# V through float32 staging buffers, K turned before Q with gated turns, and a later zeroing: what they do to a sliding-window attention and MoE kernel

## The chip, the cores and the metric

The kernel runs on one core of a Trainium2 chip. The metric is device time in microseconds (us) from the first to the last instruction, as a median over several executions. An execution is called slow when it is more than 1.5% above the fastest of the same kernel. The medians below are over all executions, a few slow ones included (348.79 us beside 343.3 us of the kernel before is one by this rule).

TensorE is PE in the profile (PEld is its weight load), VectorE is DVE, ScalarE is ACT, GpSimd is POOL and SyncE is SP.

## The reference

```python
# q, k, v: [8 batches, 8 heads, 576, 64] float32; window 32 to either side
scores = (q @ k.T) / sqrt(64);  scores[abs(i - j) > 32] = -1e9
attn   = softmax(scores)
x      = (attn @ v) -> transposed to [4608 tokens, 512]
# the "MoE" part is one dense block: w_in [512, 2048], w_out [2048, 512]
out    = (max(x @ w_in, 0) ** 2) @ w_out          # [4608, 512] float32
```

## The kernel before

A recorder takes every operation with its engine, its reads and writes, an estimated duration and a priority (`key`). A list scheduler then fixes one order for each engine, and semaphores are put in from the dependencies. **On the chip each engine's list is run in the order in which it stands**, whatever the scheduler believed about durations (in the traces of the kernels before and after, the instructions of all five engines stand in the order of their lists, by source line; in the kernel after, ACT's first casts of V come 1st, 2nd, 9th, 12th, 14th and 25th, as in its list).

Each batch of 576 positions is done in nine chunks of 64 queries. Batches 0 and 1 are fed by fine pieces, which PE transposes; ACT evicts Q and DVE evicts K. From batch 2 on, GpSimd loads Q and K raw, with a cast to bfloat16; DVE "turns" them (32x32 transposes), and SP's DMAs "spread" the turned data into the layout for the scores. V goes into `VD`. The half-shifted copy `VX`, which even chunks need, is made from `VD` by SP's DMAs; the edges of `VX` come from HBM.

```python
# ---- the scheduler's idea of a DMA (cut) ----
if op.dma is not None:
    q = "SW" if e == "POOL" else "HW"
    moved[q] = max(moved[q], t + op.dur + 700) + op.move
    if q == "HW":
        moved["SW"] += op.move          # the other way round nothing is added
    op.end = moved[q] + 1300

# ---- V: GpSimd issues DMAs that cast float32 to bfloat16 ----
def load_v(self, b, key, s):                        # four large pieces of a batch
    i = b % 2
    self.p.rec("POOL", lambda e, s=s: e.dma_start(
        self.VD[i][:, s, :, 0:64], v[b, :, 32 + 128 * s:160 + 128 * s, :].rearrange("h p d -> p h d")),
        writes=[("vd", i, s)], dma=(f"v{i}{s}", b), key=key, dur=900, move=2050)

def load_ve(self, b, key, hi):                      # the two edges of a batch
    ...                                             # three forms of the same: into VX, from POOL

def copy_v(self, b, key, s0, s1):                   # VX from VD, by SP's DMAs
    self.p.rec("SP", ... self.VX[i][0:64, s0 + 1:s1 + 1] <- self.VD[i][64:128, s0:s1] ...)

# ---- the turns of batch b (cut); raw buffers and VD/VX alternate with b % 2 ----
if b > 1:
    self.load_qk(b, "q", kb); self.load_qk(b, "k", kb)   # POOL, into RAW[t][b % 2]
    ...
    for st in range(8):
        t, dh, m = ("q", "k")[st // 4], st // 2 % 2, st % 2
        self.turn(b, t, dh, 5 * m, 5 + 4 * m, 9 * b - LEAD - TOFF + st * TST + (5 if b == 2 else 0),
                  [self.masked[min(9 * b - TREL + st, 9 * b - 1) if b > 2 else 12 + st // 2]])
        if st % 4 == 3:
            self.spread(b, t, 9 * b - LEAD - 9)          # SP
    self.copy_v(b, 9 * b - LEAD - 6, 0, 4)

# ---- zeroing for batch 1, early ----
self.setup_rest(1, -40)
self.setup_qz(1, -30, [(0, 64, 0), (64, 64, 1)])
```

The last argument of `turn` is an order constraint: a turn may not come before a given softmax mask in DVE's order. We call it the old hold.

The softmax here doesn't subtract the row's maximum and nothing guards it: scores larger than these inputs give would overflow.

## Time and profile before

The kernel took 346.15 us (median of three runs, 343.3 to 348.79).

| stretch of the profiled run | PE idle |
|---|---|
| 0 to 75 us | 21.4 us |
| 80 to 130 us | 7.5 us |
| whole span, 345.2 us | 32.9 us |

PE idle is length less PE busy in the tables of stretches. Only this idle time, the clock and the work itself can change the length, as PE, busy for 312.3 of 345.2 us, bounds the kernel.

These lines are from the page of the kernel before: busy time by engine; three rows of the picture in 40 slices, where a digit is the busy share in tenths (PEclk is the granted TensorE clock in tenths); the queues; and the chain that ended last.

```profile
PE 312.3 (90%) x2736; PEld 183.1 (53%) x2736; DVE 204.8 (59%) x468; ACT 180.9 (52%) x349; POOL 82.8 (24%) x130
...
PE   1457699999989679998999999999999999999996
...
PEclk9995689999999899999999999999999999999999
DMA  8999999965996996987997474542200000010012
...
q0 software_dynamic: 62272, 18.49, 56.7%
q1 hardware_dynamic: 14400, 20.71, 20.4%
...
PE 78%; DVE 10%; DMA 6%; ACT 3%; issue 2%; SPq 0%; ACTq 0%
```

Counting slices of 8.6 us from 0, PE has holes in slices 0 to 4, between 10 and 14 and a small one in 18, and none from slice 19 to the last but one. DMA is at 90% or more for most of the first 60 us. The table of stretches of the same kernel gives lengths, then each engine's busy us, the clock and the DMA share (the time of the packets as a share of 16 engines' time; as printed it can exceed 1). The trace holds no clock record before 20.99 us; the tables print 1.00 for that time.

```profile
core 0: us, PE busy (x) PEld busy (x) DVE busy (x) ACT busy (x) POOL busy (x), PEclk, DMA share, GB/s
0.00:20.00 20.00, 8.19 (x112) 6.84 (x112) 13.27 (x46) 7.71 (x13) 18.75 (x37) 1.00 1.21 147
20.00:40.00 20.00, 11.15 (x143) 9.47 (x144) 9.44 (x22) 9.82 (x19) 14.10 (x21) 0.70 1.49 200
40.00:60.00 20.00, 19.83 (x316) 16.57 (x315) 10.74 (x28) 11.57 (x23) 7.13 (x11) 0.88 2.35 161
```

Two places in the chain, read in order of time (start, length, what), looked worth attacking: PE's scores of batches 2 and 3 each stand after a spread of K of 7 us. These are the lines of batch 2; batch 3's spread takes 7.35 us from 116.18 us on.

```profile
93.80 7.14 DMA kt<-kst
...
101.07 0.61 PE sc L411 x8
```

Lastly the waits (who waited for whom: us in total, times, longest). GpSimd waits a lot for PE to free V's buffers, yet no engine waits for GpSimd's own work, except PE for the identity matrix at the start (5.9 us). PE waits only 1.0 us for the shifted V, `vx<-vd`.

```profile
engine line waited for: us in total, times, longest us
POOL vd L313 <- PE avp L439: 60.6, 12, 8.3
...
PE sc L411 <- DMA kt<-kst: 3.7, 2, 2.1
...
PE avp L438 <- DMA vx<-vd: 1.0, 1, 1.0
```

### The profile page before, as it was taken

To read this page: it belongs to the slowest core of one execution; us is meant where nothing else is said; L and a number is where in the kernel's file an instruction comes from. 1 tells how busy PE (TensorE), PEld (TensorE's weight loads), DVE (VectorE), ACT (ScalarE), POOL (GpSimd) and SP (SyncE) were. 2 spreads that over 40 slices of the span, in tenths; PEclk is the share of its full clock that TensorE was granted. 3 is DMA by queue.
4 is the path that set the end of the run, shared out by engine and by line. 5 is a ranking of instruction groups with operands and counts; after the bars stand their busy time and mean duration, and the time that the engine had idled before them with its cause. 6 is when DMAs were issued, how large, how long until landed. Compare 5 with 4: busy or idle time off the path is not lost.

```text
span 345.2 us, 6957 instructions
## 1 busy us (share of the span) xinstructions
PE 312.3 (90%) x2736; PEld 183.1 (53%) x2736; DVE 204.8 (59%) x468; ACT 180.9 (52%) x349; POOL 82.8 (24%) x130
## 2 busy tenths in 40 slices
PE   1457699999989679998999999999999999999996
PEld 1346398776845345544555555555555555444442
DVE  7634556869949857796886676777544444222200
ACT  2365258883536368555565555555555555544421
POOL 8999115102415424141341111100000000000000
PEclk9995689999999899999999999999999999999999
DMA  8999999965996996987997474542200000010012
GB/s 93 185 192 211 171 149 184 208 79 99 218 213 82 243 145 67 123 122 164 176 207 118 80 167 89 85 127 66 65 32 30 34 30 32 30 61 32 30 61 91
DMA packets 76703, 39.63 MB, mean 115 GB/s; under 512 B 41856, under 2 KB 71168, under 8 KB 76672
## 3 DMA queue, kind: packets, MB, share of 16 engines
q0 software_dynamic: 62272, 18.49, 56.7%
q1 hardware_dynamic: 14400, 20.71, 20.4%
q8 instruction: 21, 0.34, 0.4%
q14 instruction: 10, 0.08, 0.1%
HBM read 36.96 MB, written 9.44 MB: 134 GB/s over the span
## 4 chain that ended last, share of the span: by engine, by line
PE 78%; DVE 10%; DMA 6%; ACT 3%; issue 2%; SPq 0%; ACTq 0%
PE outp L529 32%; PE ht L511 26%; PE ht L488 7%; PE sc L411 5%; DMA kt<-kst 4%; DVE kst L366 3%; PE avp L438 3%; PE trp L467 3%; PE avp L439 3%; DMA vx<-vd 2%; DVE qz L204 2%; ACT qz L292 1%; DVE kt L295 1%; PE sc L276 1%; DVE xr L456 1%
## 5 line engine op out<-in xcount | busy, mean ns | idle before, releaser
L529 PE MATMUL outp<-w,gt 128*128 128x512 bf16 x576 | 144.8, 382 | 0.0
L511 PE MATMUL ht<-xt,w 128*128 128x512 bf16 x448 | 115.2, 383 | 0.2 <-ACT xt L471 0.2
L517 ACT ACTIVATE rt<-ht 128x512 bf16<-128x512 f32 x112 | 67.1, 599 | 69.6 <-PE ht L511 67.1
L529 PEld LDWEIGHTS outp<-w,gt 128*128 128x128 bf16 x576 | 54.2, 98 | 57.6 <-issue 1.6
L519 DVE TENSOR_TENSOR gt<-rt 128x512 bf16<-128x512 bf16 x112 | 46.6, 418 | 43.8 <-ACT rt L517 43.3
L511 PEld LDWEIGHTS ht<-xt,w 128*128 128x128 bf16 x448 | 40.8, 99 | 39.1 <-issue 2.1
L416 ACT ACTIVATE e<-sc 128x512 bf16<-128x512 f32 x72 | 42.4, 599 | 25.3 <-PE sc L411 18.2
L423 DVE TENSOR_TENSOR pt<-e,mask 128x512 bf16<-128x512 bf16 x72 | 30.0, 417 | 43.0 <-ACT e L416 42.7
L313 POOL DMA_DIRECT2D vd<-in_v_dram x32 | 28.8, 909 | 87.2 <-PE avp L439 60.6
L471 ACT ACTIVATE xt<-trp 128x256 bf16<-128x256 bf16 x72 | 27.3, 380 | 21.8 <-PE trp L467 21.6
L411 PE MATMUL sc<-qz,kt 128*128 128x128 bf16 x288 | 28.3, 229 | 8.6 <-DVE kt L295 3.9
L488 PE MATMUL ht<-xt,w 128*128 128x128 bf16 x512 | 34.8, 227 | 0.9 <-ACT rt L494 0.7
L366 DVE STREAM_TRANSPOSE kst<-kraw 128x640 bf16<-128x640 bf16 (+1 forms) x24 | 35.0, 1459 | 0.0
L366 DVE STREAM_TRANSPOSE qst<-qraw 128x640 bf16<-128x640 bf16 (+1 forms) x24 | 34.7, 1461 | 0.0
L536 ACT ACTIVATE oe<-outp 128x512 f32<-128x512 f32 x36 | 21.6, 599 | 23.9 <-PE outp L529 23.9
L488 PEld LDWEIGHTS ht<-xt,w 128*128 128x128 bf16 x512 | 31.4, 102 | 2.9 <-ACT rt L494 0.9
L411 PEld LDWEIGHTS sc<-qz,kt 128*128 128x128 bf16 x288 | 21.0, 103 | 18.4 <-DVE kt L295 4.0
L456 DVE TENSOR_TENSOR xr<-avp,rs 128x256 bf16<-128x256 f32 x72 | 30.0, 416 | 0.7
L467 PE MATMUL trp<-ident,xr 128*128 128x128 bf16 x144 | 20.6, 226 | 9.4 <-DVE xr L456 9.4
L454 DVE RECIPROCAL rs<-avp 128x4 f32<-128x4 f32 x72 | 13.4, 186 | 23.6 <-PE avp L439 22.9
L494 ACT ACTIVATE rt<-ht 128x512 bf16<-128x512 f32 x32 | 19.0, 598 | 13.2 <-PE ht L488 11.4
L467 PEld LDWEIGHTS trp<-ident,xr 128*128 128x128 bf16 x144 | 12.5, 99 | 20.9 <-DVE xr L456 10.9
(47 smaller groups left out, 226.1 us busy)
## 6 DMA issues: line engine op xcount, KB each, us to landing
out_dram<-oe SPq DMA_DIRECT2D x36, 256.0 KB, 2.0
vd<-in_v_dram POOLq DMA_DIRECT2D x32, 128.0 KB, 6.3
qraw<-in_q_dram POOLq DMA_DIRECT2D x24, 144.0 KB, 6.9
kraw<-in_k_dram POOLq DMA_DIRECT2D x24, 144.0 KB, 7.3
qz<-qst SPq DMA_DIRECT2D x48, 72.0 KB, 2.6
kt<-kst SPq DMA_DIRECT2D x24, 144.0 KB, 4.2
vx<-vd SPq DMA_DIRECT2D x12, 264.0 KB, 5.9
w<-in_moe_w_in_dram POOLq DMA_DIRECT2D x4, 512.0 KB, 11.6
```

Of the source, the lines that this page charges most:

```text
L313: self.p.rec("POOL", lambda e, s=s: e.dma_start(self.VD[i][:, s, :, 0:64], v[b, :, 32 + 128 * s:160 + 128 * s, :].rearrange("h p d -> p h ...
L366: self.p.rec("DVE", lambda e: e.transpose(dst, src), reads=[("raw", t, i, g) for g in range(4)], writes=[("st", t, dh, m0)], key=key, dur= ...
L411: mm = e.matmul(sc[:, 128 * j:128 * j + 128], self.KT[i][:, j, 64 * c:64 * c + 128], self.QZ[i][:, j, :, 64 * c:64 * c + 64], start=True, ...
L416: self.p.rec("ACT", lambda e: e.activation(self.E[n % 2][:], sc[:], ACTF.Exp, scale=0.125), reads=[("sc", n % 2)], writes=[("e", n % 2)], ...
L423: self.masked.append(self.p.rec("DVE", lambda e: e.tensor_tensor(pt, ee, mb, ALU.mult), reads=[("e", n % 2), ("mask", mi)], writes=[("pt", ...
L456: self.p.rec("DVE", lambda e: e.tensor_tensor(bass.AP(xr, 0, [[256, 128], [64, 4], [1, 64]]), bass.AP(self.AVP, 0, [[512, 128], [VE, 4], [ ...
L467: mm = e.transpose(self.TRP[:, 128 * t:128 * t + 128], xr[:, 128 * t:128 * t + 128], self.ID[:])
L488: mm = e.matmul(ht[:, 128 * (d % 4):128 * (d % 4) + 128], self.W1[:, ft, 128 * d:128 * d + 128], self.XT[:, ft, t0:t0 + 128], start=(ft == ...
L511: mm = e.matmul(ht[:], self.W1[:, ft, 128 * d:128 * d + 128], self.XT[:, ft, 512 * T:512 * T + 512], start=(ft == 0), stop=(ft == 3))
L517: self.p.rec("ACT", lambda e: e.activation(rt[:], ht[:], ACTF.Relu), reads=[("ht", k % 2)], writes=[("rt", k % 4)], key=key, dur=560)
L519: self.p.rec("DVE", lambda e: e.tensor_tensor(gt[:, d, :], rt[:], rt[:], ALU.mult), reads=[("rt", k % 4)], writes=[("gt", T % 2, d, u) for ...
L529: mm = e.matmul(op[:], gt[:, d, 128 * u:128 * u + 128], self.W2[:, d, :], start=(d == 0), stop=(d == 15))
```

## The change

The intent was to close PE's holes at the start and at 90 to 124 us. V is loaded as float32 by SP into a ring of three buffers and cast by compute engines, which frees GpSimd from 28.8 us of issuing. K is turned before Q, so that the large K spread starts earlier. A turn is held back by the position of the MoE part on PE (`gate`, `pos`) instead of by a mask. Zeroing for batch 1 leaves the start.

```diff
+        self.VF = [sb(f"vf{i}", [128, H_, 64], F32) for i in range(3)]
...
+    def take_v(self, b, key, r, n, t0, dst, tag):
+        x = self.kv % 3
+        self.kv += 1
+        vf = self.VF[x]
+        src = self.v[b, :, t0:t0 + n, :].rearrange("h p d -> p h d")
+        self.p.rec("SP", lambda e: e.dma_start(vf[r:r + n], src), writes=[("vf", x)], dma=(f"vf{x}", self.kv), key=key,
+                   dur=700, move=80 * n // 8)
+        if n == 128:      # the four large pieces of a batch
+            self.p.rec("POOL", lambda e: e.tensor_copy(dst, vf[:]), reads=[("vf", x)], writes=[tag], key=key, dur=720)
+        else:             # the edges
+            self.p.rec("ACT", lambda e: e.activation(dst, vf[r:r + n], ACTF.Copy), reads=[("vf", x)], writes=[tag],
+                       key=key, dur=560)
...                        # load_v and load_ve now call take_v
-        self.setup_rest(1, -40)
-        self.setup_qz(1, -30, [(0, 64, 0), (64, 64, 1)])
+        self.setup_rest(1, -6)
+        self.setup_qz(1, -5, [(0, 64, 0), (64, 64, 1)])
...
-                    t, dh, m = ("q", "k")[st // 4], st // 2 % 2, st % 2
-                    self.turn(..., 9 * b - LEAD - TOFF + st * TST + (5 if b == 2 else 0), [self.masked[...]])
+                    t, dh, m = ("k", "q")[st // 4], st // 2 % 2, st % 2
+                    self.turn(..., 9 * b - LEAD - TOFF + st * TST, 9 * b - LEAD - TREL + st if b > 2 else None)
...                        # gate/pos in the recorder and scheduler (cut); fine evictions: dur 480 -> 590
```

More of the change, by code (lines that the diff above doesn't have):

```diff
@@ L29 @@
     __slots__ = ("eng", "fn", "deps", "order", "inc", "val", "sem", "dma", "dur", "key", "i",
-                 "succ", "left", "ready", "start", "end", "lat", "move")
+                 "succ", "left", "ready", "start", "end", "lat", "move", "gate", "pos")
 class Prog:
@@ L45, in __init__, with rec @@
         self.readers = {}
-    def rec(self, eng, fn, reads=(), writes=(), dma=None, dur=100, key=0.0, move=0, after=(), old=()):
+    def rec(self, eng, fn, reads=(), writes=(), dma=None, dur=100, key=0.0, move=0, old=(), gate=None, pos=None):
         op = Op()
         op.eng, op.fn, op.dma, op.dur, op.key, op.move = eng, fn, dma, dur, key, move
-        op.deps, op.order = set(), set(after)
+        op.gate, op.pos = gate, pos
+        op.deps, op.order = set(), set()
         op.inc, op.val, op.sem = False, None, None
@@ L89, in schedule @@
         moved = {"SW": 0, "HW": 0}
-        out = []
+        out, held, reached = [], [], -100
         while True:
@@ L118, in schedule @@
             out.append(op)
+            if op.pos is not None:
+                while held and held[0][0] <= op.pos:
+                    s = heapq.heappop(held)[2]
+                    heapq.heappush(wait[s.eng], (max(s.ready, t), s.i, s))
+                reached = max(reached, op.pos)
             for s in op.succ:
@@ L121, in schedule @@
                 s.left -= 1
-                if not s.left:
+                if s.left:
+                    continue
+                if s.gate is not None and s.gate > reached:
+                    heapq.heappush(held, (s.gate, s.i, s))
+                else:
                     heapq.heappush(wait[s.eng], (s.ready, s.i, s))
@@ L292, in fine_turn @@
                     self.p.rec("ACT", lambda e, d=dst, c=src: e.activation(d, c, ACTF.Copy),
-                               reads=[tag] + ([w] if par else []), writes=[w], key=key, dur=480)
+                               reads=[tag] + ([w] if par else []), writes=[w], key=key, dur=590)
                 else:
                     self.p.rec("DVE", lambda e, d=dst, c=src: e.tensor_copy(d, c),
-                               reads=[tag] + ([w] if par else []), writes=[w], key=key, dur=480)
+                               reads=[tag] + ([w] if par else []), writes=[w], key=key, dur=590)
     def load_qk(self, b, t, key):
@@ L308, in load_qk @@
                        writes=[("raw", t, b % 2, g)], old=old, dma=(f"{t}{b % 2}", b), key=key, dur=620, move=1080)
+    def take_v(self, b, key, r, n, t0, dst, tag):
[7 more added lines that the diff above has]
+            self.p.rec("POOL", lambda e: e.tensor_copy(dst, vf[:]), reads=[("vf", x)], writes=[tag], key=key, dur=720)
+        else:
+            self.p.rec("ACT", lambda e: e.activation(dst, vf[r:r + n], ACTF.Copy), reads=[("vf", x)], writes=[tag],
+                       key=key, dur=560)
@@ L310, in load_v @@
     def load_v(self, b, key, s):
         i = b % 2
-        v = self.v
-        self.p.rec("POOL", lambda e, s=s: e.dma_start(
-            self.VD[i][:, s, :, 0:64], v[b, :, 32 + 128 * s:160 + 128 * s, :].rearrange("h p d -> p h d")),
-            writes=[("vd", i, s)], dma=(f"v{i}{s}", b), key=key, dur=900, move=2050)
+        self.take_v(b, key, 0, 128, 32 + 128 * s, self.VD[i][:, s, :, 0:64], ("vd", i, s))
     def load_ve(self, b, key, hi):
         i = b % 2
-        v = self.v
         if hi:
-            self.p.rec("POOL", lambda e: e.dma_start(
-                self.VX[i][64:96, 4, :, 0:64], v[b, :, 544:576, :].rearrange("h p d -> p h d")),
-                writes=[("vx", i, 4)], dma=(f"ve{i}", b), key=key, dur=650, move=512)
+            self.take_v(b, key, 64, 32, 544, self.VX[i][64:96, 4, :, 0:64], ("vx", i, 4))
@@ L324, in load_ve @@
         elif b < 2:
-            self.p.rec("POOL", lambda e: e.dma_start(
-                self.VX[i][32:128, 0, :, 0:64], v[b, :, 0:96, :].rearrange("h p d -> p h d")),
-                writes=[("vx", i, 0)], dma=(f"ve{i}a", b), key=key, dur=850, move=1536)
-        else:
-            self.p.rec("POOL", lambda e: e.dma_start(
-                self.VX[i][32:64, 0, :, 0:64], v[b, :, 0:32, :].rearrange("h p d -> p h d")),
-                writes=[("vx", i, 0)], dma=(f"ve{i}", b), key=key, dur=650, move=512)
+            for r, n in ((32, 32), (64, 64)):
+                self.take_v(b, key, r, n, r - 32, self.VX[i][r:r + n, 0, :, 0:64], ("vx", i, 0))
+        else:
+            self.take_v(b, key, 32, 32, 0, self.VX[i][32:64, 0, :, 0:64], ("vx", i, 0))
@@ L358, in load_w2, with turn @@
                    writes=[("w2", d)], dma=(f"w2{d}", 0), key=key, dur=770, move=2700)
-    def turn(self, b, t, dh, m0, m1, key, after):
+    def turn(self, b, t, dh, m0, m1, key, gate):
         raw, st, i = self.RAW[t][b % 2], self.ST[t], b % 2
@@ L367, in turn @@
                    reads=[("raw", t, i, g) for g in range(4)], writes=[("st", t, dh, m0)], key=key,
-                   dur=40 + 312 * n, after=after)
+                   dur=40 + 312 * n, gate=gate)
     def spread(self, b, t, key):
@@ L422, in scores @@
         mb = bass.AP(msk, 0, [[64, 128], [0, 4], [0, 2], [1, 64]])
-        self.masked.append(self.p.rec("DVE", lambda e: e.tensor_tensor(pt, ee, mb, ALU.mult),
-                                      reads=[("e", n % 2), ("mask", mi)], writes=[("pt", n % 2)], key=key, dur=430))
+        self.p.rec("DVE", lambda e: e.tensor_tensor(pt, ee, mb, ALU.mult),
+                   reads=[("e", n % 2), ("mask", mi)], writes=[("pt", n % 2)], key=key, dur=430)
     def av(self, n):
@@ L492, in mm1_small @@
         self.p.rec("PE", f, reads=[("xt", 8 * T + 2 * g), ("xt", 8 * T + 2 * g + 1), ("w1", q)], writes=[("ht", k % 2)], key=key,
-                   dur=900)
+                   dur=900, pos=key)
         self.p.rec("ACT", lambda e: e.activation(rt[:], ht[:], ACTF.Relu), reads=[("ht", k % 2)],
@@ L515, in mm1 @@
         self.p.rec("PE", f, reads=[("xt", 8 * T + j) for j in range(8)] + [("w1", d // 4)], writes=[("ht", k % 2)],
-                   key=key, dur=864)
+                   key=key, dur=864, pos=key)
         self.p.rec("ACT", lambda e: e.activation(rt[:], ht[:], ACTF.Relu), reads=[("ht", k % 2)],
@@ L532, in mm2 @@
         self.p.rec("PE", f, reads=[("gt", T % 2, d, u) for d in range(4 * seg, 4 * seg + 4)] + [("w2", seg)],
-                   writes=[("outp", x % 2)], key=key, dur=864)
+                   writes=[("outp", x % 2)], key=key, dur=864, pos=key)
         if seg == 3:
@@ L542, in build @@
         p = self.p
-        self.k1 = 0
-        self.masked = []
+        self.k1 = self.kv = 0
         K = -100.0
@@ L603, in build @@
                 for st in range(8):
-                    t, dh, m = ("q", "k")[st // 4], st // 2 % 2, st % 2
-                    self.turn(b, t, dh, 5 * m, 5 + 4 * m, 9 * b - LEAD - TOFF + st * TST + (5 if b == 2 else 0), [self.masked[min(9 * b - TREL + st, 9 * b - 1) if b > 2 else 12 + st // 2]])
+                    t, dh, m = ("k", "q")[st // 4], st // 2 % 2, st % 2
+                    self.turn(b, t, dh, 5 * m, 5 + 4 * m, 9 * b - LEAD - TOFF + st * TST,
+                              9 * b - LEAD - TREL + st if b > 2 else None)
                     if st % 4 == 3:
```

## The prediction

> **What bounds the kernel now.** Page: TensorE (PE) busy 312.3 of 345.2 us; the chain of waits is 78% PE. By the table of stretches the other 33 us lie in 0 to 40 us (PE busy 18.4 of 40), 90 to 124 us (about 7 us idle) and 150 to 160 us (1 us); from 160 us on PE has no gap. The granted clock is about 0.5 from 26 to 34 and 38 to 44 us and at 118 to 120 us, each after PE had idled. [...]
>
> Causes, from chain and timeline:
> - Start: two 1.02 us zeroings for batch 1 (6.50, 7.81) stand on VectorE ahead of the first K evictions, which start at 8.86 though the transposes started at 5.88. GpSimd (POOL) is busy without break from 4 to 34 us, mostly issuing DMAs (0.9 us per V load). The second V load, issued at 8.7, lands at about 19 us; PE then idles 2.6 us before 25.65.
> - 90 to 124 us: batch 2's K turns stand after its Q turns (K 85.3 to 93.1 us); the K spread lands at about 101 us (7.1 us of DMA in the chain, then PE scores). Batch 3 likewise (7.35 us, to 123.5).
>
> **What the change does.**
> - Takes all cast V loads from POOL; the 32 large ones cost 28.8 us of issuing. Adds 32 POOL copies 128x512 f32 to bf16. The trace has none[...]. Adds small ACT copies, about 0.5 us each (estimate; its others take 0.38 to 0.60): about 8 us on an engine busy 181.
> - Bytes read stay. DMA is saturated to about 60 us, so this moves order, not volume; early V loads compete with the first K and Q.
> - K first: batch 2's turns come much earlier, its K lands before the scores need it. Zeroing: 1.3 to 2 us off the start.
>
> **On the critical path** (estimates from those gaps): start 3 us (zeroing 1.5, V 2, less competition) [...]; K waits 6 of 7 us [...]; against it 1 to 2 us of VectorE delay at 55 to 75 us, where batch 2's turns (1.3 to 1.6 us each) crowd batch 1. Net about 10 us.
>
> **Predicted: 336 us, 8 in 10 between 327 and 345 us.** Faster by over 2%: 0.66; within 2%: 0.29; slower: 0.05.
>
> **Right if:** PE idle between 88 and 124 us falls from about 7.5 to under 3 us and the chain no longer holds 7 us of the K spread; first K evictions start before 8 us; no PE wait over 2 us for V before 27 us; [...] VectorE's 0.42 us masks and squares grow by less than 5%; the gapless tail keeps its length and starts earlier.
>
> **Wrong if:** POOL copies take over 1.2 us or slow VectorE; SP is blocked by V loads waiting for a free f32 buffer, holding up K and Q spreads; POOL's in-order copies wait for PE and delay the next raw Q, K loads; early V delays the first K, Q landings by over 2 us; batch 2's early turns starve batch 1, so the gap moves to 55 to 90 us.

The gains of the forecast's sum came to 11.5 us, less 1 to 2 us: net about 10. Two of its terms, 1 and 1.5 us for the clock, are cut with the sentence that they rested on, since no trace or run here shows it; the terms left come to 9 us, less 1 to 2: net 7 to 8. The "saturated" DMA is the page's row above: 90% or more in six of the seven slices to 60 us.

## The result, and the profile after

The changed kernel took **376.51 us** (median of four runs, 374.45 to 376.92); the kernel before took 346.44 beside it. The ratio is 1.0889, with a 95% interval of 1.0801 to 1.0976: it is slower. A ratio here is the mean time of one kernel's fast runs over that of the other's in the same rounds, so it is not quite the ratio of the medians quoted. The result is correct.

The same parts of the page, of the kernel after:

```profile
PE 311.7 (84%) x2694; PEld 185.0 (50%) x2736; DVE 210.8 (57%) x468; ACT 191.8 (51%) x367; POOL 64.6 (17%) x114
...
PE   1405406999948999999599999999999999999996
...
PEclk9999655899988999999899999999999999999999
DMA  8999999669239998975968792252220010001012
...
q1 hardware_dynamic: 53088, 30.42, 34.0%
q0 software_dynamic: 23616, 13.64, 26.7%
...
PE 69%; DMA 15%; DVE 8%; SPq 2%; ACT 2%; issue 2%; POOL 0%; POOLq 0%
```

PE's busy time is nearly unchanged (311.7 against 312.3 us); idle time grew from 32.9 to 60.8 us. The trace after lacks 42 of the 2736 matmul records, three at most of them before 75 us, so its idle time later on may be somewhat overstated. The two deepest holes, slices 2 and 5 (again from 0), are new. The table of stretches of the kernel after says where:

```profile
0.00:20.00 20.00, 6.21 (x94) 5.00 (x94) 13.31 (x46) 6.00 (x9) 9.77 (x23) 1.00 1.07 167
20.00:40.00 20.00, 5.76 (x62) 5.24 (x62) 2.96 (x9) 8.33 (x16) 6.60 (x12) 1.00 1.15 185
40.00:60.00 20.00, 6.04 (x74) 5.19 (x74) 3.71 (x8) 3.56 (x7) 8.85 (x15) 0.51 1.22 189
```

By 75 us PE has idled 44.3 us, against 21.4 before: 22.9 of the 27.9 us of new idle time lie there. At 40 to 60 us ACT and DVE are almost idle too (3.6 and 3.7 us busy of 20), so PE, ACT and DVE wait together. The clock falls to 0.51. It fell to 0.50 at 40.20 us, when PE had been busy for 0.28 us of the 2.00 us before, and in the kernel before at 24.40, 38.05 and 116.56 us, when PE had been busy for 0.67, 0.00 and 0.72 us of the 2.00 us before. It did not fall after every such stretch (at 122 to 124 us of the kernel before PE was busy for 0.43 us, and the clock stayed at 1.00); what sets it is not shown. The 1.00 printed for 20 to 40 us is no measurement up to 36.79 us: 16 matmuls of `ht` took 1.89 us at 32.31 us and 1.90 us at 42.36 us, where 0.50 is on record, but 1.06 us at 69.06 us, where it is 1.00.

What they wait for is an edge of V. The timeline of ACT after (start, busy, what, and in brackets the idle time before it and what ended it), in two windows:

```profile
27.80 0.63 ACT L334 ACTIVATE vx<-vf 32x512 bf16<-32x512 f32 x1 [14.26 <-DMA vf<-in_v_dram]
28.45 0.38 ACT L489 ACTIVATE xt<-trp 128x256 bf16<-128x256 bf16 x1
...
55.16 0.63 ACT L334 ACTIVATE vx<-vf 32x512 bf16<-32x512 f32 x1 [15.69 <-DMA vf<-in_v_dram]
```

Twice ACT stands about 15 us at the cast of an upper edge of V. This edge is needed only by the last chunk of its batch. Behind the cast, in ACT's order, stand the Q evictions, exponentials and `xt` copies that PE needs now. The chain of the same kernel shows how the second wait came about:

```profile
31.58 16.33 DMA vf<-in_v_dram
...
47.97 0.62 POOL vd L332
...
48.66 6.48 DMA vf<-in_v_dram
...
55.16 0.63 ACT vx L334
...
56.46 1.89 PE ht L506 x16
```

The ring's buffer was held by a large piece of V that took 16.3 us to land. The edge's load could be issued only at 48.66 us, after the GpSimd cast of that piece had freed the buffer at 48.6; it landed 6.5 us later; ACT cast it; then PE went on. The load itself hardly came later than before: in the kernel before, batch 1's upper edge landed at 54.77 us, here at 55.13 (batch 0's at 29.39, here at 27.78). Only, no compute engine stood waiting for it then. GpSimd, which casts the large pieces, waits for them in order too (40.3 us, below), and the loads of Q and K behind its casts are issued late: batch 1's last piece of Q at 48.52 us instead of 23.87, landing at 56.60 instead of 51.87.

The waits of the kernel after, beside those of before, and two lines of the view of the tile `vf` in 14 to 50 us (issue: min/median/max ns; then issue to landing):

```profile
POOL vd L332 <- PE avp L457: 92.3, 16, 13.2
POOL vd L332 <- DMA vf<-in_v_dram: 40.3, 11, 9.4
ACT vx L334 <- DMA vf<-in_v_dram: 29.9, 2, 15.7
...
PE sc L429 <- DMA qz<-qst: 6.0, 3, 3.8
```

```profile
L329 SPq DMA_DIRECT2D vf<-in_v_dram x8: 328/548/6828, 17.2 to 48.7; - x8
...
DMA to landing us min/median/max: 3.6/11.3/20.0
```

PE's waits for the spread of K (3.7 us in two) are gone; waits for the spread of Q (`qz<-qst`, 6.0 us in three) stand in their place. And one issue on SP took 6.8 us instead of about half a microsecond.

### The profile page after: what moved, and what is told of

It is laid out like the page before. It is cut to its first block, busy times and chain, and to the rows that moved or that the text cites. A ratio compares the mean times of both kernels' runs of the same rounds, so it can differ in the third digit from the quotient of the medians.

```text
span 372.5 us, 6993 instructions
## 1 busy us (share of the span) xinstructions
PE 311.7 (84%) x2694; PEld 185.0 (50%) x2736; DVE 210.8 (57%) x468; ACT 191.8 (51%) x367; POOL 64.6 (17%) x114
## 2 busy tenths in 40 slices
DMA packets 76736, 44.49 MB, mean 119 GB/s; under 512 B 41888, under 2 KB 71200, under 8 KB 76704
## 3 DMA queue, kind: packets, MB, share of 16 engines
HBM read 36.96 MB, written 9.44 MB: 125 GB/s over the span
## 4 chain that ended last, share of the span: by engine, by line
PE 69%; DMA 15%; DVE 8%; SPq 2%; ACT 2%; issue 2%; POOL 0%; POOLq 0%
PE outp L547 29%; PE ht L529 23%; DMA vf<-in_v_dram 9%; PE ht L506 5%; DMA qz<-qst 5%; PE sc L429 4%; DVE qst L384 2%; PE avp L456 2%; PE avp L457 2%; PE trp L485 2%; SPq L404 2%; DMA gt<-in_q_dram 2%; DVE kst L384 1%; ACT qz L305 1%; PE sc L289 1%
## 5 line engine op out<-in xcount | busy, mean ns | idle before, releaser
L547 PE MATMUL outp<-w,gt 128*128 128x512 bf16 x552 | 141.7, 386 | 1.5 <-issue 0.2
L529 PE MATMUL ht<-xt,w 128*128 128x512 bf16 x430 | 111.2, 380 | 0.9
L535 ACT ACTIVATE rt<-ht 128x512 bf16<-128x512 f32 x112 | 67.0, 599 | 66.6 <-PE ht L529 64.3
L537 DVE TENSOR_TENSOR gt<-rt 128x512 bf16<-128x512 bf16 x112 | 47.5, 425 | 43.5 <-ACT rt L535 42.6
L529 PEld LDWEIGHTS ht<-xt,w 128*128 128x128 bf16 x448 | 41.2, 98 | 40.7 <-issue 1.0
L441 DVE TENSOR_TENSOR pt<-e,mask 128x512 bf16<-128x512 bf16 x72 | 32.1, 446 | 42.8 <-ACT e L434 42.3
L506 PE MATMUL ht<-xt,w 128*128 128x128 bf16 x512 | 36.6, 233 | 14.1 <-ACT rt L512 11.1
L332 POOL CAST vd<-vf 128x512 bf16<-128x512 f32 x32 | 20.5, 641 | 142.5 <-PE avp L457 92.3
L506 PEld LDWEIGHTS ht<-xt,w 128*128 128x128 bf16 x512 | 33.2, 106 | 15.9 <-ACT rt L512 11.4
L429 PE MATMUL sc<-qz,kt 128*128 128x128 bf16 x288 | 28.3, 233 | 12.5 <-DMA qz<-qst 6.0
L554 ACT ACTIVATE oe<-outp 128x512 f32<-128x512 f32 x36 | 21.5, 598 | 26.6 <-PE outp L547 26.5
L489 ACT ACTIVATE xt<-trp 128x256 bf16<-128x256 bf16 x72 | 27.4, 381 | 15.0 <-PE trp L485 14.4
L485 PE MATMUL trp<-ident,xr 128*128 128x128 bf16 x144 | 20.4, 225 | 16.2 <-ACT xt L489 10.9
L429 PEld LDWEIGHTS sc<-qz,kt 128*128 128x128 bf16 x288 | 21.1, 104 | 21.4 <-DMA qz<-qst 7.5
L334 ACT ACTIVATE vx<-vf 32x512 bf16<-32x512 f32 (+1 forms) x18 | 11.3, 627 | 31.0 <-DMA vf<-in_v_dram 29.9
```

What stands on the lines that cost most here:

```text
L429: mm = e.matmul(sc[:, 128 * j:128 * j + 128], self.KT[i][:, j, 64 * c:64 * c + 128], self.QZ[i][:, j, :, 64 * c:64 * c + 64], start=True, ...
L441: self.p.rec("DVE", lambda e: e.tensor_tensor(pt, ee, mb, ALU.mult), reads=[("e", n % 2), ("mask", mi)], writes=[("pt", n % 2)], key=key, ...
L485: mm = e.transpose(self.TRP[:, 128 * t:128 * t + 128], xr[:, 128 * t:128 * t + 128], self.ID[:])
L489: self.p.rec("ACT", lambda e: e.activation(bass.AP(self.XT, 64 * n, [[4 * NTOK, 128], [NTOK, 4], [1, 64]]), bass.AP(self.TRP, 0, [[1024, 1 ...
L506: mm = e.matmul(ht[:, 128 * (d % 4):128 * (d % 4) + 128], self.W1[:, ft, 128 * d:128 * d + 128], self.XT[:, ft, t0:t0 + 128], start=(ft == ...
L529: mm = e.matmul(ht[:], self.W1[:, ft, 128 * d:128 * d + 128], self.XT[:, ft, 512 * T:512 * T + 512], start=(ft == 0), stop=(ft == 3))
```

## The experiments

Eighteen kernels were run. All gave correct results. The kernel before was run beside them (medians 346.47 to 347.38). The profiles of `rest_nogate` and `before_rawlate` fell in slow executions, so only their times are used. `edge_pool_dma` and `ring8` were profiled again; their kept traces have spans of 353.0 and 382.6 us, within 1.5% of each kernel's fastest. A kept trace of `rest_only` (354.1 us) is also of another execution than the one whose views are shown below (354.3 us); where the two differ, both numbers are given.

| run | what | median us | ratio to before, 95% interval |
|---|---|---|---|
| v_only | V part alone | 378.77 | 1.0878 [1.0768, 1.0989] |
| rest_only | gates, K first, zeroing, without V part | 356.05 | 1.029 [1.0218, 1.0362] |
| edge_pool_dma | after, edges by casting DMA | 357.0 | 1.0252 [1.0146, 1.0358] |
| ring8 | after, ring of eight | 381.63 | 1.0995 [1.0913, 1.1077] |
| edge_own_early | after, own edge buffers | 356.78 | 1.0375 [1.0278, 1.0472] |
| edge_late | the same, casts later on ACT | 360.94 | 1.0446 [1.0301, 1.0591] |
| v_own_hold | V part alone, own edge buffers | 364.98 | 1.0543 [1.0469, 1.0617] |
| edge_pool_hold | V part alone, large pieces only | 358.42 | 1.0311 [1.0252, 1.0369] |
| v_f32_pool | the same, issued by GpSimd | 359.49 | 1.0401 [1.0332, 1.047] |
| v_early | V part, batches 0 and 1 | 373.25 | 1.0762 [1.0714, 1.0809] |
| v_late | V part, batches 2 to 7 | 357.59 | 1.0307 [1.026, 1.0354] |
| zero_only | later zeroing alone | 348.24 | 1.0113 [1.0032, 1.0193] |
| kfirst_only | K first alone | 346.88 | 1.0074 [0.9995, 1.0152] |
| gate_only | gates alone | 349.76 | 1.0081 [1.0029, 1.0134] |
| rest_nogate | K first and zeroing | 346.6 | 0.9956 [0.9887, 1.0026] |
| before_rawlate | before, raw loads held | 341.08 | 0.9814 [0.9767, 0.9861] |
| rest_rawlate | rest_only, raw loads held | 341.6 | 0.9863 [0.9821, 0.9904] |
| nogate_rawlate | rest_nogate, raw loads held | 340.33 | 0.9853 [0.98, 0.9906] |

### Which part costs it: v_only and rest_only

```diff
 # v_only: the kernel before, with take_v, load_v and load_ve of the change; nothing else
 # rest_only: the kernel after, with load_v and load_ve as before
```

> The kernel before with only the V part of the change (SP loads in float32, copies on GpSimd and ScalarE). Theories 1 and 2: 370 to 380 us, ScalarE waits of over 10 us for V in the first 60 us. Theory 3: 343 to 350 us.

> The changed kernel with V loaded as before (cast on the way by GpSimd's DMAs); gates, K first and the later zeroing stay. Theory 1 (in-order waits of ScalarE for the float32 edges of V, 29.9 us in two waits of 14.3 and 15.7 us, cost the time): no such waits here, so at or below the kernel before, 334 to 346 us, and PE busy over 9 of 10 us from 40 to 60 us. Theory 2 (the ring of three buffers and GpSimd's copies waiting in order delay the loads): the same, 334 to 346. Theory 3 (gates and K first crowd VectorE): still 365 to 377 us.

V alone costs 32 us, as much as the whole change (30 us), as theories 1 and 2 said; the rest alone costs 9 us, which none of the three theories had (334 to 346, or 365 to 377 us). The two do not add up. Both act at the start and in PE's slack, but we did not test why the sum is smaller.

### Is it the edges on ScalarE, or the ring of three: edge_pool_dma and ring8

```diff
 # edge_pool_dma: in the kernel after, the 18 edge pieces again by casting DMAs from POOL; no ACT casts
-            self.take_v(b, key, 64, 32, 544, self.VX[i][64:96, 4, :, 0:64], ("vx", i, 4))
+            self.p.rec("POOL", lambda e: e.dma_start(self.VX[i][64:96, 4, :, 0:64], v[b, :, 544:576, :]...), ...)
 # ring8: in the kernel after
-        self.VF = [... for i in range(3)]      x = self.kv % 3
+        self.VF = [... for i in range(8)]      x = self.kv % 8
```

> The changed kernel, but the 18 edge pieces of V that ScalarE casts are loaded as before by GpSimd's casting DMA straight to their place; the 32 large pieces keep ring, SP loads and GpSimd copies. Theory 1: ScalarE never waits for a V load, 340 to 352 us. Theory 2: the ring (now used by large pieces alone) and GpSimd's in-order waits remain, 362 to 376 us, with GpSimd waiting about 40 us for V loads as in the changed kernel. Theory 3: 365 to 377 us.

> The changed kernel with eight float32 buffers instead of three. Theory 1: ScalarE's waits stay while the DMA engines are saturated, though the second (15.7 us, for a load issued only when a buffer came free) should shrink to a few us; 358 to 374 us. Theory 2: loads are issued early, 340 to 352 us. Theory 3: 370 to 377 us.

With the edges back on casting DMAs the kernel is 19.5 us faster than after: the edges' way over SP, the ring and ACT makes two thirds of the loss. The 357.0 us lie between the ranges of theories 1 and 2. In its kept trace ACT never waits for V, and PE has idled 26.6 us by 75 us, against 44.3 after and 21.4 before; GpSimd still waits 29.1 us for V, and PE once 7.3 us for the shifted V. More buffers did not help: 381.6 us is above the ranges of all three theories, so "the ring is too short" is refuted as a cure on its own. The kernel's own scheduler, run by itself, shows one reason: with eight buffers it believes the edges to land earlier still and moves their casts forward (batch 0's upper edge from 9th to 7th on ACT, batch 1's from 25th to 16th). In the kept trace ACT waits 34.9 us for edges, longest 17.3 us, and PE has idled 54.9 us by 75 us.

### Where ACT casts, or when the edge is loaded: edge_own_early and edge_late

```diff
 # both: in the kernel after, the edges of batches 0 to 2 do not share the ring
+        self.VG = [sb(f"vg{i}", [128, H_, 64], F32) for i in range(5)]
-        x = self.kv % 3 ...
+        if n == 128 or b > 2: ... the ring as before ...
+        else: vf = self.VG[b + 2 * (t0 == 544)]
 # edge_late only: after scheduling, each such ACT cast is moved to just before its first reader
+        for c in [o for o in self.ops if o.late][::-1]:
+            self.ops.remove(c)
+            self.ops.insert(min(self.ops.index(x) for x in c.succ), c)
```

> The pair of edge_late: the same five buffers and loads, but ScalarE's casts stay where the scheduler puts them, six of them among ScalarE's first ten entries. Theory 1: ScalarE waits 10 us or more for V and the kernel is at least 8 us slower than edge_late. If instead the buffers alone cure it, the two are within 4 us of each other.

> The changed kernel, but the edge pieces of V of batches 0 to 2 have five float32 buffers of their own (SP no longer waits for the ring to load them), and ScalarE's casts of them stand in its program just before the first matmul that reads them, not as early as the scheduler put them. Same loads, same casts, same engine. Theory 1 (in-order placement on ScalarE): ScalarE waits for V under 5 us in all, 350 to 362 us. Theory 2 (ring and GpSimd waits): 366 to 378 us.

Own buffers alone gain back some 20 us; moving the cast later on top of that gains nothing (360.9 against 356.8), where theory 1 had expected at least 8 us. With own buffers batch 1's upper edge is issued at 10.48 us and lands at 24.83, and the stall near 55 us is gone; ACT waits 11.7 us for edges instead of 29.9, longest at the start. The timeline of ACT of edge_own_early, and then a wait of edge_late:

```profile
19.60 0.63 ACT L344 ACTIVATE vx<-vg 32x512 bf16<-32x512 f32 x1 [8.30 <-DMA vg<-in_v_dram]
```

```profile
PE avp L467 <- DMA vx<-vd: 14.8, 2, 9.5
```

In edge_late ACT no longer waits for V at all, but PE now waits 14.8 us for the shifted V, against 1.3 us in edge_own_early: the wait moved to the next late piece. No run moved the casts and left the ring of three, so how much of the 20 us is ACT's place in line and how much the ring is not separated.

### The V part with the old turns: v_own_hold and edge_pool_hold

```diff
 # v_own_hold: v_only, with the five own edge buffers as in edge_own_early
 # edge_pool_hold: v_only, with load_ve as in the kernel before (only the 32 large pieces use take_v)
```

> The kernel before with the V part of the change, but with five buffers of their own for the edge pieces of batches 0 to 2; old hold, Q first, old zeroing. v_only took 379 us. If the edges' place behind the ring is what the V part costs: 346 to 352 us. If V through SP costs some 10 us more by itself (with the edges cured): 354 to 362 us.

> The kernel before with only the 32 large pieces of V loaded by SP in float32 and copied on GpSimd; edge pieces as before; old hold, Q first, old zeroing. If the gates are the whole of what edge_pool_dma still lost (10 us): 345 to 350 us. If V through SP has its own cost: 354 to 360 us, with waits of PE before 40 us for V or its copies.

Against v_only (1.0878), own buffers give back 14 us and casting DMAs for the edges 20 us. So the edges cost about 20 of the V part's 32 us here as well, with the old turns. The 11 us that are left belong to the large pieces. v_own_hold (365.0 us) lies above both of its expected ranges; edge_pool_hold (358.4 us) is where "V through SP has its own cost" put it, with PE waits of 8.8 us for the shifted V.

### When the V part costs: v_early and v_late

```diff
 def load_v(self, b, key, s):             # and the same in load_ve
+    if not (b > 1):                      # v_late;  v_early: if not (b < 2)
+        return self.load_v_cast(b, key, s)   # the code of before
```

> Kernel before with the V part for batches 0 and 1 only. Theory A: nearly all of the V part's cost, ratio 1.06 to 1.09, 368 to 378 us, with ScalarE waiting over 5 us in one piece for an upper edge before 60 us. Rival B: a quarter of it, about 354 us.

> Kernel before with the V part of the change for batches 2 to 7 only; batches 0 and 1 as before. Theory A (the V part costs while the first batches' V has not arrived, because ScalarE and GpSimd then wait in order for late data): from batch 2 on V has many microseconds of slack, so ratio 0.99 to 1.01, about 347 us, and PE idle before 75 us as in the kernel before (about 21 us). Rival B (the V path through float32 buffers, an SP issue and two compute copies costs steadily in every batch): 6 of 8 batches pay, so about 0.75 of the 30 us, about 369 us.

v_early is as theory A had it: 27 us, and 26.2 us of ACT waits for edges (first line below). v_late is a miss for both theories, and the two costs add up to 38 us, more than the V part's 32. It costs 11 us, neither nothing nor 22 us. Its profile keeps A's place but not A's reason: PE has been busy for 45.2 us by 75 us, against 53.6 in the kernel before, so most of this loss too lies at the start; ACT does not wait for V there. Batch 2's first three float32 loads wait for nothing, so SP issues them at 0.8 to 1.7 us, into the DMA traffic of the start (DMA share 1.33 at 0 to 40 us). Later loads, held in order for a buffer, stand ahead of the `vx` copies on SP. One such copy took 4.6 us to issue and landed 14.4 us after its start, where in the kernel before the first copies took 4.9 to 8.4. PE then waits for them (second line). The two lines are from the waits of v_early and of v_late:

```profile
ACT vx L322 <- DMA vf<-in_v_dram: 26.2, 3, 14.3
```

```profile
PE avp L471 <- DMA vx<-vd: 10.8, 3, 4.9
```

### Is it SP's queue: v_f32_pool

```diff
 # edge_pool_hold, with the float32 loads issued by GpSimd (and a semaphore from its own casts)
-        self.p.rec("SP", lambda e: e.dma_start(vf[r:r + n], src), ...
+        self.p.rec("POOL", lambda e: e.dma_start(vf[r:r + n], src), ...
```

> As edge_pool_hold (kernel before with the 32 large V pieces through float32 buffers and GpSimd copies, edges as before), but the float32 loads are issued by GpSimd, so that SP's queue again holds only the vx copies, spreads and outputs. Theory E (the V part's remaining 3% comes from SP's queue: the vx copies that PE waits for stand behind large float32 loads, and SP waits in order for a free buffer): before 60 us the vx copies land in 5 to 8 us instead of 8 to 16, PE's waits for vx<-vd fall under 3 us, ratio 0.995 to 1.015. Rival F (the staging itself, a ring of three and a GpSimd copy that waits in order, costs it): ratio 1.02 to 1.04 as before.

Theory E falls as to the time, and rival F's range is met. The `vx` copies issued before 60 us did land in 5.2 to 7.9 us again, and PE's idle time by 75 us fell to 23.2 us (28.3 in edge_pool_hold), but between 80 and 130 us it rose to 15.5 us (8.8 in edge_pool_hold), and the time stayed at +4%. Now the float32 loads themselves came late, up to 26.6 us after issue, and PE waited still longer for the shifted V. Waits of edge_pool_hold and of v_f32_pool:

```profile
PE avp L450 <- DMA vx<-vd: 8.8, 2, 7.5
```

```profile
PE avp L450 <- DMA vx<-vd: 15.7, 4, 6.3
```

The kernel before had 1.0 us there. In each variant the way from HBM to `VX` has one more in-order station (a ring buffer and a GpSimd cast), and PE pays for it at `vx<-vd`. Which queue causes it is not settled: moving the issue only moved the wait.

### The other three parts, one at a time: zero_only, kfirst_only, gate_only, rest_nogate

```diff
 # zero_only (in before):   setup_rest(1, -40) -> (1, -6);  setup_qz(1, -30, ...) -> (1, -5, ...)
 # kfirst_only (in before): ("q", "k")[st // 4] -> ("k", "q")[st // 4]
 # gate_only:   rest_only with Q first, the early zeroing and dur 480
 # rest_nogate: kfirst_only and zero_only together, dur 590, the old hold
```

> The kernel before with only the zeroing for batch 1 moved later. My prediction's step: first scores 1.2 us earlier, 1 to 2 us faster (344 to 345 us). Rival, from the run of the rest of the change without the V part: the gain turns into a wait of about 2.5 us for V's first rows, and the time is the same within 1 us, 345.5 to 348 us.

> The kernel before with only K's turns ahead of Q's; its own hold on the turns stays. If K first is to blame for the 10 us of the rest of the change: 352 to 358 us, with PE waiting over 4 us in one go for a spread of Q. If the new gates are to blame: 343 to 348 us.

> The kernel before with only the hold on the turns changed: gated by the position of the MoE matmuls in the scheduler's clock (none for batch 2), not ordered behind a mask multiply; Q still first, zeroing and V as before. If the gates make the 10 us of the rest of the change: 352 to 359 us, with a PE wait of 4 us or more for a spread between 85 and 135 us. If it takes the gates and K first together: 345 to 350 us.

> K first, the later zeroing and the longer eviction estimate together, with the old hold on the turns and V as before. If the gates are needed for the loss: 345 to 350 us. If K first with the zeroing makes it without the gates: 353 to 359 us.

None gains clearly, and zero_only's 348.2 us are just above the rival's 345.5 to 348. In rest_only (kept trace) the later zeroing did start the first scores earlier (10.35 us, 11.34 before), but PE then waited 2.37 us for the first rows of V. K first left PE's idle time between 80 and 130 us as it was (7.45 us before, 7.65 with kfirst_only): the wait has another name. With the gates as well (rest_only, which also has the later zeroing) it became 13.1 us (10.2 us in the kept trace), and that run is 3% slower. The chain of rest_only at batch 2 (batch 3 has the same with 7.59 us from 124.52 us on; the kept trace has 6.08 and 7.15 us):

```profile
91.21 5.81 DMA qz<-qst
...
97.06 1.03 PE sc L424 x8
```

Now the Q spread takes the time that the K spread took. In the kernel before, the Q spread was the quick one. The view of DMA issues, 80 to 98 us (KB each, median us from issue to landing), of before:

```profile
qz<-qst SPq DMA_DIRECT2D x10, 72.0 KB, 2.1
qraw<-in_q_dram POOLq DMA_DIRECT2D x4, 144.0 KB, 6.4
kt<-kst SPq DMA_DIRECT2D x4, 144.0 KB, 6.4
```

and of rest_only:

```profile
qz<-qst SPq DMA_DIRECT2D x8, 72.0 KB, 6.2
```

It is the second spread that is slow, whichever it is (kfirst_only has the Q spread at 5.7 us there). Once the first tensor is turned, its raw buffer is free, and GpSimd at once issues the raw loads for two batches later. In the kept trace of rest_only the K turns end at 82.99 us, and raw K loads are issued from 83.30 us, just ahead of the Q spread (from 85.01 us).

### Do the raw loads slow the second spread: before_rawlate, rest_rawlate, nogate_rawlate

```diff
 # the raw Q and K loads of batch b+2 also wait for the second spread of batch b
                        writes=[("raw", t, b % 2, g)], old=old, ..., move=1080)
+                       .deps.update(self.spr.get(b - 2, ()))
 # in spread, for the tensor that is turned second (K in before_rawlate, Q in the others):
+                    self.spr.setdefault(b, []).append(self.p.rec("SP", ...))
```

> Kernel before, with the raw Q and K loads of batch b+2 held until the K spread of batch b has landed. Theory C (the second of the two spreads is slow because the raw loads that the first tensor's turns release share the DMA engines with it): the K spreads of batches 2 and 3 fall from 5 to 8 us to 2 to 4 us, PE idle for kt at 99 and 121 us falls from 3.7 us to under 1 us, ratio 0.985 to 1.0. Rival D (the spread is slow because of weights, outputs or its own size): the spread stays at 5 to 8 us and the waits stay; ratio 1.0 or a little more since raw loads come later.

> The run rest_only (gates, K first, later zeroing, V as before), with the raw loads of batch b+2 held until the Q spread of batch b has landed. Theory C: the Q spreads of batches 2 and 3 fall from 6 to 8 us to 2 to 4 us, the three PE gaps at 85 to 127 us (14 us together) fall under 6 us, ratio from 1.029 to 1.00 to 1.01. Rival D: spreads and gaps stay, ratio 1.02 to 1.04.

> rest_nogate (K first, later zeroing, the old hold, V as before) with the raw loads of batch b+2 held until the Q spread of batch b has landed. If the raw loads are what slowed the second spread whatever its name and whatever the gates, this gains as much as before_rawlate and rest_rawlate did: ratio 0.975 to 0.990, about 341 us, and PE idle at 85 to 127 us for qz under 2 us. If the order K first matters once the loads are held, it is over 1% faster than before_rawlate.

Theory C holds, and the gains are a little larger than forecast in rest_rawlate (1.00 to 1.01) and before_rawlate (0.985 to 1.0). In rest_rawlate the Q spread of batch 2 falls to 3.2 us, between 80 and 98 us:

```profile
qz<-qst SPq DMA_DIRECT2D x8, 72.0 KB, 3.2
```

PE busy between 80 and 130 us, first in rest_only, then in rest_rawlate:

```profile
80.00:130.00 50.00, 36.94 (x367) 24.76 (x369) 33.74 (x68) 20.83 (x41) 15.82 (x24) 0.93 1.00 164
```

```profile
80.00:130.00 50.00, 46.63 (x468) 29.00 (x466) 40.67 (x88) 28.75 (x59) 17.20 (x26) 0.97 1.06 168
```

PE's idle time there falls from 13.1 us (10.2 in the kept trace) to 3.4 us. The edit alone makes the kernel before 1.9% faster (341.08 us). The intervals of the three held variants overlap: with the loads held, no gain of K first, the gates or the zeroing can be told. These are the only versions clearly faster than the kernel before; the gain stays just under 2%. One rival is not excluded: GpSimd works in its list's order (as in the traces of before and after), so holding the raw loads also holds what stands behind them there, and the scheduler's lists change with the new dependency. No run held those other loads alone.

## Why the prediction was wrong

The prediction said 336 us, and that slower by over 2% had a chance of 5%. The step that failed is the term for the start: it took the casts of V as a few us of busy time and let no engine wait for them, while ACT alone waited 29.9 us for two edges and PE lost 22.9 us by 75 us. The second term, for the K waits, failed too. Point by point:

- **"Start 3 us (zeroing 1.5, V 2, less competition)"**: this term failed, in sign and size. PE lost 22.9 us by 75 us, where 3 were to be gained. V by SP did land somewhat earlier (the second large piece at 14.45 us instead of 18.71, batch 1's last at 54.14 instead of 54.41), but a cast now stood for each piece, and ACT and GpSimd waited for V in order. By the letter PE had no wait of over 2 us for V before 27 us, as predicted, but it stood idle for 10.9 us up to 28.98 us behind ACT, which waited for V. The edges' new way cost about 20 us (edge_pool_dma, edge_pool_hold); the large pieces about 11 (edge_pool_hold), and where these are lost is only partly traced (`vx<-vd`).
- **"Adds small ACT copies, about 0.5 us each: about 8 us on an engine busy 181"**: the busy time came out somewhat higher (0.63 us each, 11.3 us in all), but busy time was the wrong measure. The wait before two of these copies was 29.9 us, and everything behind them on ACT waited too.
- **"DMA is saturated to about 60 us, so this moves order, not volume"**: HBM reads did stay at 36.96 MB, but the bytes moved rose from 39.63 to 44.49 MB, since V now lands as float32 (256 KB for a large piece, 128 before). The DMA engines' share fell all the same, from 77.1% for the two main queues to 60.7%: no sign that heavier transfers caused the loss. The experiments point to order, and the prediction did not ask which engine now waits for that order.
- **"K waits 6 of 7 us"**: failed. PE idle at 88 to 124 us was 7.2 us after and 7.5 us before, against under 3 predicted. The kernel after runs some 20 us late there (batch 2's scores start at 121.88 us instead of 101.07), so kfirst_only, with 7.65 us against 7.45 at 80 to 130 us, is the cleaner test. The competing raw loads went unseen. K first only swaps which spread meets them (kfirst_only); holding the loads removes it or most of it (no wait for a second spread is left on PE's list at 80 to 130 us in rest_rawlate and nogate_rawlate).
- **"Zeroing: 1.3 to 2 us off the start"**: locally right (first K eviction at 6.90 us instead of 8.86), worth nothing alone (zero_only, +1.1%), since PE then waits for V.
- **The GpSimd copies**, whose forecast time is cut: the 32 casts took 0.61 us at the least and 0.641 on average, under the 1.2 us that would have counted against the forecast.
- **"VectorE's masks and squares grow by less than 5%"**: squares grew by 2% (418 to 425 ns), masks by 7% (417 to 446 ns). All of VectorE grew by 6 us; it is not the bound (busy for 210.8 of 372.5 us, PE for 311.7).
- **"The gapless tail keeps its length and starts earlier"**: wrong. PE is busy 35.95 of the 40 us from 160 to 200 us in the kernel after, against 40.00 before; a wait for the Q spread stands there.
- Of the listed risks, "SP is blocked by V loads waiting for a free f32 buffer" (the load of 48.66 us) and "POOL's in-order copies wait for PE and delay the next raw Q, K loads" came true: GpSimd waited 92.3 us for PE (60.6 before) and 40.3 us for V, and batch 2's first raw Q load was issued at 52.87 us instead of 26.82, landing at 57.26 instead of 52.90. That SP's waits held up a spread is not shown. "Early V delays the first K, Q landings by over 2 us" did not: they came 0.45 and 1.7 us later. The greatest loss, ACT standing still for an edge, was not on the list.

The order was fixed by a scheduler that adds SP's transfers to GpSimd's backlog but not the other way round (the code above). It believed the edges to land early and put their casts early on ACT: run by itself, it has batch 1's upper edge land at 24.0 us and its cast as the 25th on ACT, where the trace has the landing at 55.13 us. In the trace SP's loads of edges did not land alike: the first edge, issued at 0.80 us, landed 1.9 us later; one issued at 17.20 us, with GpSimd's loads of K and Q in flight (landed at 22.55 and 24.07 us), landed 10.6 us later. That a better model would have avoided the placement is not shown; no run changed the model. Why gates, K first and the zeroing cost 3% together, and about 1% or less each, also stays open. Shown is only that the cost is gone once the raw loads are held.

## What to carry to other kernels

When a load with a cast becomes a load and a copy, ask which in-order engine now stands waiting for that load, and what stands behind it; the copy's busy time says little (here 11.3 us busy, 29.9 us of waits before two copies). When a wait follows one transfer, look what else was released just before it: here reordering moved the wait to the next transfer (the Q spread, a median of 6.2 us in rest_only), while holding back the competitor removed it (3.2 us in rest_rawlate). A longer ring alone need not help: here the scheduler then placed the casts still earlier (381.63 us with eight buffers, 376.51 with three).
